# Attention and a feed-forward layer on one core: a planner in the kernel takes over the order of all engines

## The chip, the cores and the metric

The kernel runs on one core of one Trainium2 chip. Such a core has a matrix engine (TensorE, PE in the profile), three engines for everything else (VectorE is DVE, ScalarE is ACT, GpSimd is POOL), a queue engine (SyncE, SP) and 16 DMA engines that move data between HBM and the on-chip memories SBUF and PSUM. Each engine works through its own list of instructions in order and waits on semaphores for the others. The metric is the device time of one launch in microseconds (us), lower is better.

## The reference

Four sequences of 768 positions, eight heads of 64, go through masked attention; the result (3072 rows of 512) goes through a gated feed-forward layer. Heads 0, 2 and 6 see all earlier positions; the other five ("streaming" heads) see the first 4 positions and the last 64.

```python
scores = (q @ k.T) / 8                       # per batch and head, 768 x 768
mask   = causal                              if is_retrieval[head]     # [1,0,1,0,0,0,1,0]
         causal & (pos < 4 | rel < 64)       otherwise
a      = softmax(where(mask, scores, -1e9))
x      = (a @ v) as [3072, 512]
h      = x @ w_in                            # 512 -> 2048
out    = (h * sigmoid(beta * h)) @ w_out     # 2048 -> 512
```

All inputs and the output are f32 in HBM: q, k and v of 6.3 MB each, w_in and w_out of 4.2 MB each, the output of 6.3 MB.

## The kernel before

The work is cut in 8 chunks: a batch and half of its 768 positions, in the order (batch 0, first half), (1, first), (0, second), (1, second), and the same for batches 2 and 3. A chunk is counted from 0 here, so "chunk 1" is the second. Each chunk has four units, a pair of heads (p and p+4); unit u = 4 x chunk + p. Scores are computed in blocks of 128 keys by 128 queries, only where the mask lets anything through: 43 blocks in a chunk of a first half, 75 in one of a second half, 472 in all.

What happens to a chunk, with the lines of the profile:

- Loads. k, q and v of chunk 0, 1 and 2 come as f32 over SP's queue (`load_qk` L137, `load_v` L151). The weights come over POOL's queue, which casts f32 to bf16 on the way (L161 for w_in, L165 for w_out). From chunk 3 on, the rows of k and q come over POOL's queue too, cast on the way (`load_rows` L325, 60 loads); v stays on SP.
- Getting the head dimension onto partitions. Chunks 0 to 2: cast to bf16 (L293), transpose on PE (L367), copy out of PSUM (L368, L373). From chunk 3: a DMA transpose issued by SP (L336). `KT` holds the keys, `QTP`/`QTD` the queries. POOL makes a copy `KO` of the keys with the first 4 positions put in (L350, L351), and the same for the values, `VO` from `VX` (L312, L313). `VX` is the cast v (L299).
- Scores. Chunks 0 to 2 (`steps_QK`, L458) use a matmul over 128 rows with the other head's half of the queries zeroed; chunks 3 to 7 (`scores`, L926) use matmuls over 64 rows, the two heads side by side. Chunks 0 and 1 add the mask on PE (L463); later ones multiply it on DVE after the exponential (L431). The exponential is ACT's (L466, L930), into tiles `es`.
- Values. `steps_PV` (L489) multiplies `es` with `VX`/`VO`; DVE divides (L492, L494); the result `x` is transposed to `xT` on PE (L521, L523), or by a DMA from chunk 2 on (L505).
- Feed-forward. G1 (L554) is 16 tiles of 4 matmuls per chunk, each followed by a tanh on ACT (L557) and the gate on DVE (L560), which fills `gT`. G2 (L598, the last piece L581) is 12 parts of 4 matmuls per chunk; the result is scaled (L603, L605) and stored (L608).

The order is written out by hand: a list of calls for chunks 0 and 1, one loop for chunk 2 with a count of G1/G2 steps to put in, and from chunk 3 on a string per group of scores that says where G1 ("1"), G2 ("2") and PV ("p") steps stand. Loads have hand-set times. In the list for the start, chunk 1's k, q and v loads stand directly behind chunk 0's, ahead of the weights:

```python
    cast_dp(0)
    load_v(0, held=True)
    load_qk(1, 0)
...
    load_qk(1, 1, held=True)
...
    load_v(1, held=True)
...
    load_w_in(0)
```

`held=True` puts a small POOL memset into the tile ahead of the load, so that the load waits for it. PE starts with ten matmuls on zeros (`idle`, L188).

## Time and profile before

| what | value |
|---|---|
| median of 3 runs | 238.94 us (238.83 to 239.57) |
| span of the profiled execution, first to last instruction | 235.3 us |
| median less that span | 3.6 us |
| PE busy | 222.3 us (94% of the span) |
| ACT, DVE, POOL busy | 155.3, 144.7, 103.4 us |
| bytes read from HBM, written | 27.27 MB, 6.29 MB |
| granted TensorE clock | 1.00 throughout |

The page shows one execution, and of that the span; the page gives no total of its own for this execution, so the 3.6 us around the span is the distance to the median. Busy times of different engines lie beside each other. A busy PE counts a matmul from its start to its modelled end, so closely spaced matmuls overlap in it; what a matmul takes from the next one is read from the start of one to the start of the next.

### The profile page before, as it was taken

The page shows a single profiled execution, that of the slowest core. Times are in us where ns is not written, and L with a number is a line of the kernel's source. Part 1 is how long each engine was busy: PE and PEld are TensorE (multiplying, and loading weights), DVE is VectorE, ACT ScalarE, POOL GpSimd, SP SyncE. Part 2 cuts the span into 40 slices and gives each one's busy share as a digit, 9 for nine tenths or more (in the row PEclk, how much of TensorE's full clock was granted, in tenths as well). Part 3 has the DMA queues.
Part 4 walks back from the last instruction along what each step waited for, and adds up shares of the span by engine and source line. Part 5 has one row for each costly group of instructions (what it writes and reads, how often), then busy time and mean ns, then how long its engine had stood idle before and what let it go on. Part 6 is the DMA issues. An engine that isn't in the chain of part 4 may idle for free.

```text
span 235.3 us, 5334 instructions
## 1 busy us (share of the span) xinstructions
PE 222.3 (94%) x1960; PEld 131.8 (56%) x1960; DVE 144.7 (61%) x356; ACT 155.3 (66%) x303; POOL 103.4 (44%) x230
## 2 busy tenths in 40 slices
PE   7786899999999999999799999999989999999994
PEld 3675665555555566546454565455745556555553
DVE  6768679886758389637845592444881666338700
ACT  2796788847673998657674757584927797128621
POOL 6487850199469987059899319000560000000000
PEclk9999999999999999999999999999999999999999
DMA  6999999999999999989999963156511101211012
GB/s 196 261 276 194 177 167 231 224 212 212 201 133 132 129 139 156 148 146 150 219 192 142 212 149 81 46 92 165 123 33 61 49 0 45 81 45 49 0 45 89
DMA packets 96314, 31.78 MB, mean 135 GB/s; under 512 B 82704, under 2 KB 93344, under 8 KB 96288
## 3 DMA queue, kind: packets, MB, share of 16 engines
q0 software_dynamic: 35968, 8.13, 46.7%
q1 hardware_dynamic: 59456, 22.72, 45.0%
q10 hardware_dynamic: 864, 0.60, 0.8%
q8 instruction: 15, 0.25, 0.5%
q14 instruction: 11, 0.09, 0.1%
HBM read 27.27 MB, written 6.29 MB: 143 GB/s over the span
## 4 chain that ended last, share of the span: by engine, by line
PE 60%; DMA 14%; POOL 13%; DVE 4%; issue 3%; ACT 3%; SPq 2%; POOLq 0%; ACTq 0%
PE tp L598 25%; PE mm L554 21%; POOL s L325 7%; DMA vs<-in_v_dram 6%; DMA s<-in_q_dram 5%; PE po L489 4%; PE sp L926 3%; DMA xT<-x 2%; PE mm L188 2%; DVE gT L560 2%; POOL VX L299 2%; PE tp L581 1%; PE sp L458 1%; ACT es L930 1%; POOL KO L350 1%
## 5 line engine op out<-in xcount | busy, mean ns | idle before, releaser
L554 PE MATMUL mm<-xT,w_in_sb 128*128 128x384 bf16 x512 | 92.4, 326 | 1.5 <-DMA w_in_sb<-in_moe_w_in_dram 0.9
L598 PE MATMUL tp<-w_out_sb,gT 128*128 128x512 bf16 x368 | 89.6, 379 | 0.0
L557 ACT ACTIVATE th<-mm,beta_h 128x384 f32<-128x384 f32 x128 | 73.0, 597 | 24.0 <-PE mm L554 19.4
L560 DVE SCALAR_TENSOR_TENSOR gT<-th,mm 128x384 bf16<-128x384 f32 x128 | 67.7, 550 | 32.5 <-ACT th L557 28.1
L554 PEld LDWEIGHTS <-w_in_sb 128*128 128x128 bf16 x512 | 48.1, 97 | 33.9 <-issue 2.4
L598 PEld LDWEIGHTS <-gT 128*128 128x128 bf16 x368 | 33.8, 98 | 33.9 <-issue 0.8
L930 ACT ACTIVATE es<-sp 128x512 bf16<-128x512 f32 (+1 forms) x84 | 39.9, 597 | 4.1 <-PE sp L926 4.1
L605 ACT ACTIVATE osb<-tp 128x512 f32<-128x512 f32 x21 | 12.7, 604 | 35.4 <-PE tp L598 32.1
L299 POOL CAST VX<-vs 128x384 bf16<-128x384 f32 x22 | 11.4, 522 | 38.0 <-DMA vs<-in_v_dram 38.0
L489 PEld LDWEIGHTS <-es 128*128 128x128 bf16 x472 | 20.6, 97 | 10.8 <-issue 3.5
L466 ACT ACTIVATE es<-sp 128x512 bf16<-128x512 f32 (+1 forms) x44 | 22.7, 560 | 4.6 <-PE sp L458 3.6
L489 PE MATMUL po<-VX,es 128*128 128x65 bf16 x392 | 22.5, 193 | 1.0 <-POOL VX L299 0.9
L325 POOL DMA_DIRECT2D s<-in_q_dram x30 | 22.5, 773 | 0.9 <-issue 0.7
L431 DVE TENSOR_TENSOR es<-es,Mh 128x512 bf16<-128x512 bf16 (+3 forms) x58 | 19.9, 378 | 4.5 <-ACT es L930 3.8
L325 POOL DMA_DIRECT2D s<-in_k_dram x30 | 22.4, 775 | 0.5 <-issue 0.3
L494 DVE TENSOR_TENSOR x<-po,rec 128x384 bf16<-128x384 f32 x32 | 17.8, 557 | 1.1
L458 PE MATMUL sp<-QTP,KT 128*128 128x128 bf16 (+2 forms) x113 | 16.8, 230 | 1.7 <-ACT es L466 0.9
L350 POOL COPY KO<-KT 128x128 bf16<-128x128 bf16 (+1 forms) x24 | 10.2, 423 | 13.2 <-DVE KT L368 11.2
L431 DVE TENSOR_TENSOR es<-es,Mc 128x384 bf16<-128x384 bf16 (+2 forms) x21 | 7.2, 349 | 12.7 <-ACT es L930 12.0
L492 DVE RECIPROCAL rec<-po 128x6 f32<-128x6 f32 x32 | 6.1, 192 | 13.4 <-PE po L489 13.2
L458 PEld LDWEIGHTS <-KT 128*128 128x128 bf16 x113 | 10.4, 98 | 4.1 <-issue 1.2
L293 POOL CAST qkb<-s 128x384 bf16<-128x384 f32 x12 | 6.2, 532 | 13.4 <-DMA s<-in_q_dram 13.4
(73 smaller groups left out, 173.2 us busy)
## 6 DMA issues: line engine op xcount, KB each, us to landing
vs<-in_v_dram SPq DMA_DIRECT2D x24, 256.0 KB, 6.0
out_dram<-osb SPq DMA_DIRECT2D x23, 256.0 KB, 2.4
s<-in_k_dram SPq DMA_DIRECT2D x12, 192.0 KB, 4.8
w_in_sb<-in_moe_w_in_dram POOLq DMA_DIRECT2D x8, 256.0 KB, 7.6
w_out_sb<-in_moe_w_out_dram POOLq DMA_DIRECT2D x4, 512.0 KB, 10.9
s<-in_q_dram SPq DMA_DIRECT2D x10, 192.0 KB, 5.2
s<-in_k_dram POOLq DMA_DIRECT2D x30, 64.0 KB, 5.0
s<-in_q_dram POOLq DMA_DIRECT2D x30, 64.0 KB, 5.4
```

The costliest lines, as they stand in the source:

```text
L299: copy(out=VX[b % 2, p][:, h2 * HT:(h2 + 1) * HT, :, 0:D], in_=staged["v", c][:, :, p:H:NPAIR, :])
L325: nc.gpsimd.dma_start(out=ROWS[c % 2, name][:, t].rearrange("p (a w) -> p a w", a=NPAIR)[:, :, w:w + D], in_=src[b, hh * NPAIR:(hh + 1) * ...
L431: nc.vector.tensor_mul(e, e, m)
L458: nc.tensor.matmul(sp[:, (i - lo) * 128:(j - lo) * 128], lhs, s["QT"][hh][:, q0 * 128:(q0 + j - i) * 128], start=True, stop=not added)
L466: nc.scalar.activation(out=es[:, 0:w], in_=sp[:, 0:w], func=ACTF.Exp, scale=scale)
L489: nc.tensor.matmul(po[:, qi, hh, :], e, val, start=(j == 0), stop=(j == len(lst) - 1))
L494: nc.vector.tensor_mul(x, po[:, :, :, 0:D], rec.to_broadcast([128, HT, 2, D]))
L554: nc.tensor.matmul(hp[:, 0:HALF], w_in_sb[:, mo, fi * 128:(fi + 1) * 128], xT[c][:, mo, :], start=(mo == 0), stop=(mo == MO - 1))
L557: nc.scalar.activation(out=th, in_=hp[:, 0:HALF], func=ACTF.Tanh, scale=beta_h[:, fi:fi + 1])
L560: nc.vector.scalar_tensor_tensor(out=gTs[c][:, fi, :], in0=th, scalar=1.0, in1=hp[:, 0:HALF], op0=ALU.add, op1=ALU.mult)
L598: nc.tensor.matmul(op, gTs[c][:, fi, ns * 128:(ns + 1) * 128], w_out_sb[:, fi, :], start=(fi == 0), stop=(fi == FO - 1))
L930: nc.scalar.activation(out=es[:, 0:w], in_=sp[:, 0:w], func=ACTF.Exp, scale=scale)
```

## The change

The hand-written order is gone. All work is put into a list of tasks with an engine (or a choice of engines), a cost, what they depend on, a priority and the buffers they take; a `Planner` inside the kernel runs through them with its own clock while the program is built, gives each engine the first ready task in order of priority, and so writes a fixed list for every engine. The chip sees only the finished lists. The main parts:

- **Loads.** The order is a list, `ramp`: chunk 0, then all of w_in and a quarter of w_out, then chunk 1's k and q, a quarter of w_out, chunk 1's v, the rest of w_out, and then row after row of the later chunks. A tiny POOL copy (`hold`, L407) from a tile that landed into the destination of a later load makes that load wait. `kq` in the list is a unit's k and q.
- **Later rows as f32.** From chunk 2 on (`early` is 2), k and q come over SP's queue as f32 (L541), are cast by POOL or DVE (L251) and transposed by SP's DMA (L578). POOL's 60 casting loads (L325) are gone.
- **Scores over 64 rows everywhere** (L742), from chunk 0 on; the zeroed halves are gone. Masks of chunks 0 and 1 stay on PE (L731), now up to 384 columns in one matmul. Chunks 2 to 7 are cut in smaller groups.
- **Transposes.** PE transposes k, q only for chunks 0 and 1 (L512), and `x` only for those (L824); the rest goes by DMA (L832).
- **Buffers.** All 8 PSUM banks, 24 `es` tiles and 14 staging tiles of 128x512 f32 are handed out by the planner; v is cast in whole 128-row tiles by DVE or ACT, in chunks 0 and 1 also by POOL (L249, L251).
- **Attention ahead.** Groups of scores and PV have higher priority than G1 and G2; G2 is the filler. Both second-half chunks of batches 0 and 1 are through attention before chunk 2's G1 begins.

```diff
+CFG = {'fill': 10, 'g1_banks': (5, 4, 3, 2), 'long1': [0, 9, 18, 26, 34, 42], 'es': 24, 'early': 2, 'g1_limit': 1600, ...
+class Planner:
+    def pick(self, e):
+        kept = set()
+        lst = self.ready[e]
+        lst.sort(key=lambda t: t.prio if not callable(t.prio) else t.prio(self))
+        for t in lst:
+            if t.seen or t.ready > self.now:
+                continue
...
+            got = self.tokens(t, kept)
+            if got is not None:
+                return t, got
...
+    def hold(name, trigger, box, prio, make):
...
+            nc.gpsimd.tensor_copy(out=dst[0:n], in_=src[0:n])
+        return add("H" + name, "POOL", (124, 186), go, [trigger], prio=-500 + prio, take=box)
...
+        t = add(f"L{which}{u}", e_, 450 if e_ == "SP" else 400, go, [hd], prio=5 * u + (which == "q"),
+                take=box if hd is None else None, dma=(16, 40, *hw))
...
+    ramp = cfg.get("ramp", [("kq", 0), ("kq", 1), ("kq", 2), ("kq", 3), ("v", 0), ("in", 0), ("in", 1), ("in", 2), ("in", 3),
+                            ("out", 0), ("kq", 4), ("kq", 5), ("kq", 6), ("kq", 7), ("out", 1), ("v", 1), ("out", 2), ("out", 3)])
...
+    ramp = ramp + [x for c in range(EARLY, NCHUNK) for x in (("rows", c), ("v", c))]
...
-    def load_rows(c):
...
-            nc.gpsimd.dma_start(out=ROWS[c % 2, name][:, t].rearrange("p (a w) -> p a w", a=NPAIR)[:, :, w:w + D],
+                    eng[e].dma_start(out=s, in_=src[b, :, r:r + 128, :].rearrange("h p d -> p h d"))
...
+                def turn(e, which=which, t=t, box=box):
+                    j = h2 * HALF + t * 128
+                    out_ = KTB[b % 2][:, :, j:j + 128] if which == "k" else QTD[c % 2][:, :, t * 128:(t + 1) * 128]
+                    nc.sync.dma_start_transpose(out=out_, in_=box["w"].rearrange("p a c d -> p (a c d)"))
...
+            casts.append(add(f"Cv{c}{t}", cfg.get("v_cast", ("DVE", "ACT")) if c >= EARLY else cfg.get("v_cast0", ("DVE", "ACT", "POOL")), c_copy(512, False, True), go,
+                             [ld, t_ones[b % 2, h2]] + old, prio=u_prio(4 * c, -3), gives=[lambda ld=ld: ld.got]))
...
+        t = add(f"PV{u}", "PE", c_mm(65, nb), pv, ready_es[u] + vdeps, prio=prio, take=[(banks, 1, allowed, 1)],
...
+            t = add(f"G1.{c}.{fi}", "PE", c_mm(384, 4), mm, deps + w + old, prio=pr, take=[(banks, 1, cfg.get("g1_banks", (0, 1, 2, 3, 4, 5)), 1)])
...
-                    nc.tensor.matmul(sp[:, (i - lo) * 128:(j - lo) * 128], lhs, s["QT"][hh][:, q0 * 128:(q0 + j - i) * 128],
-                                     start=True, stop=not added)
+                nc.tensor.matmul(sp[:, a * 128:z * 128], lhs[half(h)], QTD[(u // NPAIR) % 2][half(h), units[u][2], q0 * 128:(q0 + z - a) * 128],
+                                 start=not st_, stop=True, skip_group_check=bool(st_))
```

Three places of the finished lists, on which the prediction rests.

POOL's list at the start. Before, POOL issues the first w_in load among the casts of chunk 1 (`qkb` is a cast k or q, `VO`, `VX` values of a batch, `s0` a staging tile); this is a stretch of before:

```order
L313 COPY VO00_154<-VX00_152 4x64
L161 DMA w_in_sb_78<-in_moe_w_in_dram 64x4x512 x2
L293 CAST qkb_400<-s0_200 128x384
L312 COPY VO01_157<-VX01_155 128x2x64
L313 COPY VO01_157<-VX01_155 4x2x64
```

After, w_in follows the last cast of chunk 0, and the one-column copies (L407) stand ahead of each load:

```order
L251 CAST qkb_255<-st_177 128x2x3x64
L407 CAST w_in_sb_69<-st_184 128x1 x2
L471 DMA w_in_sb_69<-in_moe_w_in_dram 64x4x512 x4
L609 COPY KO03_95<-KT0_87 128x128
L612 COPY KO03_95<-KT0_87 128x4
L407 CAST w_in_sb_69<-st_207 128x1
L471 DMA w_in_sb_69<-in_moe_w_in_dram 64x4x512 x2
```

w_in moved ahead of everything of chunk 1, and each of its loads now waits for an earlier landing.

PE's list where chunk 1's first values are used (`po` is PV's result, `VX10`/`VX1` the values of batch 1, `mm` G1, `sp` scores, `tp` here G2). Before, G1 of chunk 0 and scores of chunk 1 follow it:

```order
L489 LDWEIGHTS es_515
L489 MATMUL po_661<-VO10_164,es_515 128x65
L489 LDWEIGHTS es_515
L489 MATMUL po_661<-VX10_162,es_515 128x65
L554 LDWEIGHTS w_in_sb_78
L554 MATMUL mm_677<-xT_455,w_in_sb_78 128x384
```

After, all of chunk 0's G1 and all scores of chunk 1 stand ahead of it, and the first G2 stands behind this unit's twelve PV matmuls (these are the last scores, the first PV and, further on, the last PV and the first G2):

```order
L742 MATMUL sp_792<-QTD1_86,KT1_88 128x128
L742 LDWEIGHTS KT1_88
L742 MATMUL sp_794<-QTD1_86,KT1_88 128x128
L798 LDWEIGHTS es_758
L798 MATMUL po_809<-VX1_90,es_758 128x65
```

```order
L798 LDWEIGHTS es_749
L798 MATMUL po_809<-VX1_90,es_749 128x65
L798 LDWEIGHTS es_765
L798 MATMUL po_809<-VX1_90,es_765 128x65
L923 LDWEIGHTS gT_472
L923 MATMUL tp_825<-w_out_sb_70,gT_472 128x512
```

G1 and the scores moved ahead of the first use of chunk 1's v, and no G2 stands between its last score and that use.

DVE's list where the masks of chunk 2 start (`Mc`, `Mh1` are masks). Before, the casts of chunk 3's v stand after nearly all masks of chunk 2:

```order
L431 TENSOR_TENSOR es_1369<-es_1369,Mh1_146 128x512
L299 CAST VX10_162<-vs_833 128x6x64
L299 CAST VX11_165<-vs_833 128x6x64
L299 CAST VX12_168<-vs_833 128x6x64
L299 CAST VX13_169<-vs_833 128x6x64
L431 TENSOR_TENSOR es_1393<-es_1393,Mh1_146 128x512
```

After, the first of them (`st_1130` is chunk 3's v) stands ahead of the first mask:

```order
L942 TENSOR_SCALAR osb_1196<-tp_922 128x512
L251 CAST VX1_90<-st_1130 128x8x64
L771 TENSOR_TENSOR es_1245<-es_1245,Mc_80 128x384
L771 TENSOR_TENSOR es_1248<-es_1248,Mc_80 128x256
L251 CAST VX1_90<-st_1151 128x8x64
L771 TENSOR_TENSOR es_1282<-es_1282,Mc_80 128x128
```

The cast, and with it the wait for a load of chunk 3, moved ahead of the masks of chunk 2.

## The prediction

> **What bounds the kernel now.** I read the page's head and busy times, then the busy time by stretches, then the chain of waits for the pace of each kind of matmul, then the loads.

> ```profile
> span 235.3 us, 5334 instructions
> PE 222.3 (94%) x1960; PEld 131.8 (56%) x1960; DVE 144.7 (61%) x356; ACT 155.3 (66%) x303; POOL 103.4 (44%) x230
> ...
> 0.00:36.00 36.00, 30.03 (x359) 21.55 (x360) 25.83 (x75) 25.94 (x54) 23.60 (x78) 1.00 1.08 212
> 36.00:84.00 48.00, 47.14 (x398) 27.73 (x397) 35.01 (x80) 34.75 (x68) 31.70 (x55) 1.00 1.32 180
> 84.00:132.00 48.00, 46.33 (x428) 26.84 (x423) 30.77 (x79) 32.84 (x64) 34.60 (x66) 1.00 1.84 170
> 132.00:180.00 48.00, 46.86 (x402) 26.41 (x401) 27.29 (x67) 31.86 (x65) 13.49 (x32) 1.00 0.46 104
> 180.00:232.00 52.00, 51.89 (x387) 29.30 (x385) 25.48 (x55) 29.61 (x56) 0.00 (x0) 1.00 0.12 43
> ```

> In a row by stretches stand the stretch, its length, the busy time of PE, PE's weight loads, DVE, ACT and POOL, then clock, DMA share and GB/s. From 36 us on PE is idle for 3.8 us of 196; no other engine comes near. Before 36 us it is idle for 6.0, and what is busy there is thin: 359 instructions, many of them small. So the kernel is PE's work plus what the start loses. The start waits for data: the DMA share is over 1 there.

> The chain gives what one matmul takes from the next (its columns: start, length, what):

> ```profile
> 1.29 4.45 PE mm L188 x10
> 65.95 0.33 PE tp L367 x6
> 188.96 4.55 PE mm L554 x28
> 199.54 0.52 PE po L489 x17
> 221.65 6.91 PE tp L598 x32
> 228.55 3.51 PE tp L581 x32
> ```

> G1 162.5 ns (4.55/28), G2 216 ns and in its last half-width piece 110 ns, PV 30.6 ns, a transpose 55 ns. For scores over 64 rows the sum over all stretches serves, since two run side by side: these 254 matmuls hold 311 blocks, 11.86 us, so 38.1 ns a block, with the starts of the groups in it. Over 128 rows a block takes one 128-column matmul, 55 ns.

> ```profile
> sum 236.00, PE 11.86; mean PE 0.59
> ...
> 21.23 0.22 PE L458 MATMUL sp<-QTP,KT 128*128 128x128 bf16 x1
> 21.29 0.22 PE L463 MATMUL sp<-Ns,idb 128*128 128x128 bf16 x1
> 21.34 0.22 PE L458 MATMUL sp<-QTP,KT 128*128 128x128 bf16 x1
> ...
> 0.00:36.00 36.00, 7.62 (x42) 1.00 1.08 212
> ```

> The last row is G1 alone: 42 of 512 matmuls lie in the first 36 us. PE's list shows what else remains then: all of G2, 386 PV, 24 + 9 transposes, the 75 blocks of chunk 2 over 128 rows and all 311 over 64. By the paces above: 470 x 0.1625 = 76.4, 368 x 0.216 + 32 x 0.110 = 83.0, 386 x 0.0306 = 11.8, 33 x 0.055 = 1.8, 75 x 0.055 = 4.1 and 11.9, together 189.0 us. The last matmul ends at 228.55 + 3.51 = 232.06, so 196.06 us were spent on it: 7.1 us are stalls, spread out.

> **The change, part by part.** I set the end of PE's work after the change as the time of one event, plus the work behind it, plus stalls. The event is PE's first PV of chunk 1: it needs chunk 1's v, the last load that the start needs in full, and nothing can pass it in PE's list.

> *When chunk 1's v is there.* The rates of the loads are in four stretches of the start: k and q of chunk 0 at 3 to 7 us, v at 8 to 11, weights alone at 28 to 30 and, with the passage from w_in to w_out in it, at 28 to 35.

> ```profile
> 4.08 0.55 DVE L293 CAST qkb<-s 128x384 bf16<-128x384 f32 x1
> ...
> 3.00:7.00 4.00, 3.44 (x14) 1.61 (x13) 3.02 (x19) 0.93 (x4) 2.30 (x15) 1.00 1.09 338
> 8.00:11.00 3.00, 2.48 (x45) 2.31 (x43) 2.53 (x6) 2.52 (x6) 1.44 (x6) 1.00 1.32 220
> 28.00:35.00 7.00, 6.71 (x82) 4.78 (x83) 5.25 (x13) 6.06 (x13) 4.58 (x11) 1.00 1.13 171
> 28.00:30.00 2.00, 1.81 (x29) 1.54 (x30) 1.39 (x5) 1.79 (x5) 1.88 (x6) 1.00 1.20 193
> ...
> vs<-in_v_dram SPq DMA_DIRECT2D x24, 256.0 KB, 6.0
> w_in_sb<-in_moe_w_in_dram POOLq DMA_DIRECT2D x8, 256.0 KB, 7.6
> w_out_sb<-in_moe_w_out_dram POOLq DMA_DIRECT2D x4, 512.0 KB, 10.9
> s<-in_q_dram SPq DMA_DIRECT2D x10, 192.0 KB, 5.2
> xT<-x SPq DMA_TRANSPOSE x21, 4.1
> ...
> 100.56 3.89 SPq L336 DMA_TRANSPOSE KT<-s  x3
> ```

> The weights' sizes are those of the bf16 side (8 x 256 and 4 x 512 KB make 4.2 MB for 8.4 MB of f32), and so is their rate. The first k of chunk 0 is there at 4.08. Seven more loads of 192 KB at 338 GB/s take 4.1 us, v 0.79 MB at 220 takes 3.6: 11.8 us, as before the change. Then w_in and half of w_out, 3.15 MB: 16.3 us at 193, 18.4 at 171; I take the middle, 17.3, since passages from one queue to the other occur here too. Chunk 1's k and q 1.57 MB 4.7 us, its v 3.6. That is 37.4 us (36.4 to 38.5). The casts of v and POOL's copies for the first unit cost 0.5 + 0.24 + 0.3 + 0.23: PV of chunk 1 starts at 38.7. Overlap between the queues gains nothing here, the engines being full in each of these rows.

> PE has 64 G1 matmuls (10.4), 86 blocks (3.3), masks (68 blocks of columns, 3.7), 60 transposes (3.3), 43 PV (1.3) and the ten on zeros (4.45) to do until then: 26.5 us of 37.4. It waits some 11 us in the start, where the kernel before had no such wait but had less behind it.

> *The work behind that event.* G1 448 x 0.1625 = 72.8, G2 83.0 as before, PV 429 x 0.0306 = 13.1, 12 transposes 0.7, 386 blocks x 0.0381 = 14.7: 184.3 us. Relative to before, the 64-row scores of chunks 0 to 2 take away 161 x (55 - 38) ns = 2.7 us and 33 transposes 1.8 us. In their place SP issues nine more DMA transposes (six of chunk 2's k and q, three of x), 1.3 us each (3.89 for three), and 36 row loads instead of 8 unit loads and POOL's 60; 60 transposes then hold SP for 78 us of 230, which bounds nothing by itself.

> *Stalls.* 7.1 us before. In 84 to 132 stand 1.67 us of idle PE beside a POOL that is busy for 34.6 of 48 us; the chain goes through its casting loads there:

> ```profile
> L325 POOL DMA_DIRECT2D s<-in_q_dram x30 | 22.5, 773 | 0.9 <-issue 0.7
> L325 POOL DMA_DIRECT2D s<-in_k_dram x30 | 22.4, 775 | 0.5 <-issue 0.3
> L299 POOL CAST VX<-vs 128x384 bf16<-128x384 f32 x22 | 11.4, 522 | 38.0 <-DMA vs<-in_v_dram 38.0
> ```

> These 44.9 us go; 36 casts of 512 columns come, by the casts above (522 ns for 384) about 25 us shared with DVE. I let the 1.67 us go. New waits come with the order: DVE's and ACT's casts of chunk 2's v stand amid the gates and tanhs of chunk 1, those of chunk 3's v ahead of chunk 2's masks. Bounds: nothing, if the loads are early, and 6 us (the third rival). I take 1.0, near the low end, since G2 parts without these waits stand between. Stalls: 7.1 - 1.7 + 1.0 = 6.4.

> *Costed at nothing:* the masks of chunks 0 and 1 (same columns, fewer matmuls); `x` of the last unit by DMA, whose landing (4.1 us median before) is covered by the 52 G1 and G2 matmuls of older chunks (10.4 us) ahead of chunk 7's G1, and would cost its 4.1 without them. The last store is as before.

> *Sum.* 38.7 + 184.3 + 6.4 = 229.4 against 232.06: 2.7 us less. From the span of 235.3 that is 232.6, and with the 3.6 us around it (238.94, the median, less the span) 236.3 us. Its own range: 36.4 to 38.5 for v, 3 to 8 for the stalls, 233.0 to 238.0.

> **The rivals.**

> *The start and the order are better than I think.* Weights at 193 GB/s put PV at 37.7, and if a plan with one clock for all engines leaves 3 us of stalls, the end is 37.7 + 184.3 + 3.0 = 225.0, 7.1 less: 231.9 us. For it: no engine but PE is over 66% busy. Against: the stalls before are many and small, and the finished lists cannot give way to a late load.

> *The clock.* The first ten matmuls of 512 columns took 4.45 us, where 32 later ones took 6.91: ten would be 2.2. So a matmul after a pause at the start is at half pace, for 2.3 us in all. The longest wait of PE in the trace afterwards is 0.93 us, and no slow stretch follows it. After the change 11 us of waiting collect before 38.7, most in one piece; if the pace falls again, 2.3 us come on top: 238.6, no change. [...]

> ```profile
> 23.16 1.14 PE L554 MATMUL mm<-xT,w_in_sb 128*128 128x384 bf16 x6 [0.93 <-DMA w_in_sb<-in_moe_w_in_dram]
> ```

> *Slower: chunk 3's v is late.* Place: DVE's cast of it, ahead of chunk 2's masks; behind it wait the masks, behind these PE's PV of chunk 2. After v of chunk 1 (37.4) come the rest of w_out (1.05 MB, 5.8 us at 182), k and q of chunk 2 (1.57 MB at 220: 7.1), its v (3.6), six transposes (0.13 MB each at 220: 3.6), k and q of chunk 3 (7.1) and one v (1.2): 65.8. PE comes to PV of chunk 2 after 108 G1 and G2 matmuls (64 + 44, 19.9 us), 55 small ones (2.0), chunk 2's scores (2.9) and 36 G2 (7.8): 71.3. Ten masks (378 ns) and a cast lie between, about 4 us, so 1.5 us are to spare. The loads decide it when they take 30 us instead of 28.4. For it: with both kinds of load moving, 146 GB/s in 60 to 72.

> ```profile
> 60.00:72.00 12.00, 11.55 (x119) 7.39 (x118) 8.04 (x19) 8.07 (x17) 6.62 (x12) 1.00 1.41 146
> L431 DVE TENSOR_TENSOR es<-es,Mh 128x512 bf16<-128x512 bf16 (+3 forms) x58 | 19.9, 378 | 4.5 <-ACT es L930 3.8
> ```

> At a quarter more, 35.5 us, the masks are 5.6 us late, and the end is 241.9. Against it: that row is of POOL's small casting loads, which are gone.

> **How the numbers follow.** The forecast, 236.3, has 0.42; the better start, 231.9, 0.18; the clock, 238.6, 0.15; the late v, 241.9, 0.25. Within 0.3% of 238.94 (238.2 to 239.7, about what a measurement of this kernel can tell from no change) lies only the clock: faster 0.60, same 0.15, slower 0.25. The range reaches from 230.9, a microsecond under the better case, to 241.9, the late case; what is left out is the half of the late case that is later still and a few chances in a hundred below.

> **What would show it.** The first PV of chunk 1 (L798 on VX1) at 38.7, ended by a DMA or by POOL's copies behind it; PE's busy time in the first 36 us well below 30; G1 at 162.5 ns right after, or at 325 if the clock fell; scores (L742) at 38 ns a block; waits of DVE for a v load between 50 and 70 us; and PE idle for under 2 us from 90 us on. I am wrong if PV of chunk 1 comes before 36 or after 41, if the blocks of the small groups take over 45 ns (2.7 us more), or if PE waits in the late stretches, for which I have put in no new reason.

## The result: 268.53 us, and the profile after

The changed kernel takes 268.53 us (median of 4 runs, 266.29 to 272.62) against 238.88 for the kernel before, run beside it (238.51 to 239.57): 1.121 times as long, 95% interval 1.114 to 1.127. The forecast was 236.3. The profiled execution is the longest of the four, 272.62 us with a span of 270.9 and the lowest mean clock (0.937, the others 0.949 to 0.967), so the losses read from it below are some 4 us larger than those of the median.

The head of the page, and from its slices the clock that was granted to PE:

```profile
span 270.9 us, 5159 instructions
PE 233.2 (86%) x1873; PEld 129.5 (48%) x1895; DVE 136.1 (50%) x340; ACT 158.5 (58%) x317; POOL 71.7 (26%) x205
...
PEclk9999689599999597999999995999799999999999
```

Every other engine is busy for less or about the same as before, and PE for a smaller share. Two things are new: PE has holes, and the clock falls in six places. By stretches (PE, weight loads, DVE, ACT, POOL, then clock, DMA share, GB/s):

```profile
0.00:36.00 36.00, 27.93 (x214) 14.38 (x214) 17.63 (x53) 20.68 (x44) 19.62 (x70) 0.91 0.98 198
36.00:84.00 48.00, 42.23 (x328) 22.99 (x332) 22.29 (x48) 29.23 (x63) 19.95 (x50) 0.93 0.85 164
84.00:132.00 48.00, 40.05 (x384) 23.97 (x381) 27.16 (x72) 29.80 (x61) 13.35 (x36) 0.89 0.84 174
132.00:180.00 48.00, 39.82 (x305) 21.10 (x309) 25.84 (x68) 28.45 (x56) 16.93 (x44) 0.93 0.92 170
180.00:232.00 52.00, 48.08 (x468) 28.23 (x473) 34.03 (x85) 36.16 (x72) 1.86 (x6) 0.97 0.27 60
232.00:271.00 39.00, 35.13 (x193) 18.82 (x193) 9.16 (x17) 14.15 (x25) 0.00 (x0) 1.00 0.15 55
```

Before, PE was idle for 1 to 2 us in each middle stretch; now for 6 to 8. The last matmul ends at 267.2 instead of 232.06, 35.2 us later, and this divides as follows. PE's idle time up to its last matmul is 267.2 - 233.2 = 34.0 us, where it was 232.06 - 222.3 = 9.8: 24.2 us more. In half-microsecond stretches, 34.1 us after the start-up have a granted clock of 0.50; PE is busy for 28.0 us of them, which is 14.0 us of work at full clock, so 14.0 us are lost there, and none before. 24.2 + 14.0 is 38.2; the 3.0 us less are roughly the work that the change takes away.

What PE waited for, longest sums first (total, times, longest):

```profile
PE mm L856 <- DVE gT L864: 7.3, 5, 4.1
PE mm L856 <- DMA xT<-x: 5.5, 4, 2.6
PE po L798 <- POOL VX L251: 4.1, 1, 4.1
PE tp L512 <- POOL qkb L251: 3.6, 1, 3.6
PE sp L742 <- DMA QTD<-rb: 2.5, 1, 2.5
```

Behind the lower four stands a transfer, and behind the longest wait for a gate too. One place shows how a late load stops DVE, ACT and PE; the timeline at 158 to 169 us (start, length, engine, what, and in brackets the idle time before):

```profile
156.58 1.85 DVE L864 SCALAR_TENSOR_TENSOR gT<-th,mm 128x384 bf16<-128x384 f32 x3
163.02 0.43 DVE L251 CAST VX<-st 128x512 bf16<-128x512 f32 x1 [4.59 <-DMA st<-in_v_dram]
163.96 1.44 PE L856 MATMUL mm<-xT,w_in_sb 128*128 128x384 bf16 x4 [4.13 <-DVE gT L864]
164.00 1.05 ACT L861 ACTIVATE th<-mm,beta_h 128x384 f32<-128x384 f32 x2 [4.86 <-DVE gT L864]
...
157.86 1.69 SPq L945 DMA_DIRECT2D out_dram<-osb  x1
159.60 2.13 SPq L453 DMA_DIRECT2D st<-in_v_dram  x3
```

DVE's next instruction is the cast of a v tile. SP issues that load only at 159.60, behind a run of transposes and a store. The gates behind the cast had their tanh; G1 behind the gates had its inputs; all wait, and 4.1 us later PE goes on at half clock (0.50 from 163 to 169 us).

### The profile page after: what moved, and what is told of

Read it like the earlier page. It is cut to its first block, busy times and chain, and to the rows that moved or that the text cites. A ratio compares the mean times of both kernels' runs of the same rounds, so it can differ in the third digit from the quotient of the medians.

```text
span 270.9 us, 5159 instructions
## 1 busy us (share of the span) xinstructions
PE 233.2 (86%) x1873; PEld 129.5 (48%) x1895; DVE 136.1 (50%) x340; ACT 158.5 (58%) x317; POOL 71.7 (26%) x205
## 4 chain that ended last, share of the span: by engine, by line
PE 61%; DMA 20%; POOL 4%; DVE 4%; issue 3%; ACT 3%; SPq 3%; POOLq 0%; DVEq 0%; ACTq 0%
PE tp L923 25%; PE mm L856 24%; DMA st<-in_v_dram 10%; DMA xT<-x 5%; PE po L798 5%; PE sp L742 4%; PE mm L336 2%; DMA w_in_sb<-in_moe_w_in_dram 2%; DMA st<-in_q_dram 2%; ACT es L756 1%; DMA out_dram<-osb 1%; DVE gT L864 1%; SPq L453 1%; DVE x L812 1%; DMA QTD<-rb 1%
## 5 line engine op out<-in xcount | busy, mean ns | idle before, releaser
L923 PE MATMUL tp<-w_out_sb,gT 128*128 128x512 bf16 (+1 forms) x378 | 89.4, 379 | 4.3 <-ACT osb L940 2.5
L756 ACT ACTIVATE es<-sp 128x384 bf16<-128x384 f32 (+2 forms) x144 | 63.1, 532 | 9.1 <-PE sp L742 8.7
L923 PEld LDWEIGHTS <-gT 128*128 128x128 bf16 x400 | 38.1, 100 | 44.3 <-issue 8.1
L251 POOL CAST rb<-st 128x512 bf16<-128x512 f32 (+1 forms) x44 | 23.4, 545 | 45.9 <-DMA st<-in_k_dram 30.4
L940 ACT ACTIVATE osb<-tp 128x512 f32<-128x512 f32 (+2 forms) x19 | 10.8, 569 | 31.6 <-PE tp L923 24.0
L798 PE MATMUL po<-VX,es 128*128 128x65 bf16 x392 | 22.5, 206 | 4.9 <-POOL VX L251 4.1
L798 PEld LDWEIGHTS <-es 128*128 128x128 bf16 x472 | 20.7, 107 | 11.7 <-issue 7.5
L742 PE MATMUL sp<-QTD,KT 64*128 64x128 bf16 (+2 forms) x310 | 22.0, 241 | 4.2 <-DMA QTD<-rb 2.5
L771 DVE TENSOR_TENSOR es<-es,Mh 128x384 bf16<-128x384 bf16 (+3 forms) x60 | 20.3, 376 | 1.8 <-ACT es L756 1.3
L812 DVE TENSOR_TENSOR x<-po,rec 128x384 bf16<-128x384 f32 x32 | 17.6, 551 | 4.2 <-DMA xT<-x 3.7
L742 PEld LDWEIGHTS <-KT 64*128 64x128 bf16 x310 | 12.2, 96 | 14.3 <-issue 11.8
L942 DVE TENSOR_SCALAR osb<-tp 128x512 f32<-128x512 f32 (+1 forms) x7 | 4.4, 633 | 23.8 <-ACT osb L940 18.3
L640 POOL COPY VO<-VX 128x128 bf16<-128x128 bf16 (+3 forms) x24 | 8.9, 391 | 26.8 <-DVE VX L251 15.7
L251 DVE CAST VX<-st 128x512 bf16<-128x512 f32 x16 | 7.0, 447 | 14.9 <-DMA st<-in_v_dram 14.8
L798 PE MATMUL po<-VO,es 128*128 128x65 bf16 x80 | 10.7, 213 | 0.6 <-POOL VO L643 0.5
## 6 DMA issues: line engine op xcount, KB each, us to landing
st<-in_v_dram SPq DMA_DIRECT2D x24, 256.0 KB, 4.6
out_dram<-osb SPq DMA_DIRECT2D x23, 256.0 KB, 2.2
st<-in_k_dram SPq DMA_DIRECT2D x18, 256.0 KB, 5.0
st<-in_q_dram SPq DMA_DIRECT2D x18, 256.0 KB, 5.2
w_in_sb<-in_moe_w_in_dram POOLq DMA_DIRECT2D x8, 256.0 KB, 7.0
w_out_sb<-in_moe_w_out_dram POOLq DMA_DIRECT2D x4, 512.0 KB, 6.9
st<-in_k_dram SPq DMA_DIRECT2D x8, 192.0 KB, 3.8
st<-in_q_dram SPq DMA_DIRECT2D x7, 192.0 KB, 4.0
```

The lines of the kernel that those rows point to most:

```text
L251: eng[e].tensor_copy(out=out, in_=in_)
L742: nc.tensor.matmul(sp[:, a * 128:z * 128], lhs[half(h)], QTD[(u // NPAIR) % 2][half(h), units[u][2], q0 * 128:(q0 + z - a) * 128], start=n ...
L756: nc.scalar.activation(out=es[:, 0:w], in_=sps[n_][:, 0:w], func=ACTF.Exp, scale=scale)
L771: nc.vector.tensor_mul(x, x, m)
L798: nc.tensor.matmul(po[:, qi, hh, :], e_, val, start=(j == 0), stop=(j == len(lst) - 1))
L812: nc.vector.tensor_mul(x, box["po"][:, :, :, 0:D], box["rec"].to_broadcast([128, HT, 2, D]))
```

## The experiments

Four theories were weighed, and they changed as the runs came in. W: loading the weights ahead of chunk 1 costs the time, in the start. S: SP's queue is full, and what it issues is late (S2 is the same with the two kinds of its work told apart: row loads one behind the other, and transposes behind them). D: the DMA engines are full, or the landing of 256 KB rows is the limit. P, formed after the first four experiments: the lists were laid out for loads cheaper than the chip's, so that each list asks for data before it is there. C goes with all of them: a wait is followed by a stretch at half clock, as at the six falls above, of 3.4 or 6.8 us each.

For S, the issues of SP from 48 to 192 us, summed over the trace: 54 loads of 0.98 us, 54 transposes of 1.29 us, 13 stores of 0.70, 132 us of 144. A piece of SP's timeline:

```profile
120.95 4.87 SPq L541 DMA_DIRECT2D st<-in_q_dram  x3
125.92 3.08 SPq L453 DMA_DIRECT2D st<-in_v_dram  x3
129.10 4.11 SPq L578 DMA_TRANSPOSE KT<-rb  x3
133.31 3.84 SPq L578 DMA_TRANSPOSE QTD<-rb  x3
```

**The loads on POOL's queue.**

```diff
-'late_q': 'SP'
+'late_q': 'POOL'
```

> One setting of the changed kernel is altered: the f32 rows of k, q and the v tiles of chunks 2 to 7 are issued on POOL's queue instead of SP's; bytes, casts and transposes stay. Theory S (from 48 to 192 us the SP queue itself is full: its issues sum to about 132 of 144 us there, 54 loads for 54 us and 54 transposes for 68 us, and PE waits for what SP is late with): the loads' 54 us leave SP, the transposes alone fill under half of it, most of PE's 22 us of idle after 48 us and of the half-pace behind it go: 243 to 252 us. Theory D (the DMA engines or the landing times of 256 KB f32 rows are the limit, whichever queue issues them): 264 us or more, and PE's waits after 48 us stay. Both expect the first PV of chunk 1 where it was, near 44 to 48 us.

Measured: 276.04 us (268.69 to 279.89), no gain, since even the shortest run equals the changed kernel. The number lies in D's range, but what happened is in neither theory. SP was rid of the loads, but POOL now sent them out far ahead, chunk 3's among them, while SP's transposes of chunk 2 went out, and these landed late (the last column is from issue to landing; 48 to 84 us):

```profile
KT<-rb SPq DMA_TRANSPOSE x3, 17.6
QTD<-rb SPq DMA_TRANSPOSE x3, 10.7
```

In the changed kernel the medians are 2.6 and 2.4 us in that stretch. PE waited 18.5 us for `QTD` in two pieces. What is clear: freeing SP's issue time does not by itself bring data sooner. S in its plain form is out; D isn't shown by it, since the order of the transfers changed as well.

**x transposed on PE in all chunks.**

```diff
+'x_pe': tuple(range(8, 32))
```

> The changed kernel with x of all chunks transposed on PE instead of by DMA (24 DMA transposes less on SP, 72 PE transposes and 24 evictions more). Theory S: 24 x 1.24 = 30 us leave SP between 95 and 230 us, and xT no longer stands behind row loads; PE pays 72 x 0.055 = 4.0 us: 250 to 260 us. Theory D: the waits for v and k, q rows stay, only the 5.5 us of PE waiting for xT goes against 4 us of PE work: 264 to 269 us.

Measured: 264.05 us (262.61 to 264.62), 4.5 less than the changed kernel; it lies at D's edge, 264. SP's transposes between 48 and 192 us fell from 54 to 36 and all its issues there from 132 to 105 of 144 us, but PE's idle time in that stretch only from 21.5 to 20.0 us. So PE's waits stay when SP's queue is no longer full. It waited 5.6 us for gates, and for exponentials that stand ahead of what it needs on ACT 5.5 us in G1 and 4.4 in scores.

**The old order of the first loads.**

```diff
+'ramp': [chunk 0, kq 4 to 7, v 1, w_in 0 to 3, w_out 0 to 3]
```

> The changed kernel with the old order of the first loads: chunk 1's k, q and v directly behind chunk 0's, the weights after them. Theory W (the weights ahead of chunk 1 cost the time): v of chunk 1 lands near 24 instead of 47 us, both long waits of PE in the start go (3.6 and 4.1 us) with the half clock behind them (some 5 us): 254 to 259 us. Theory S: the rows of chunk 2 still start only behind the weights, near 47 us, and what PE gains ahead of them it waits for later: 263 to 269 us.

Measured: 265.65 us (264.64 to 266.64), 2.9 less, inside S's range and far from W's. The start did what W said:

```profile
23.23 0.52 PE L798 MATMUL po<-VX,es 128*128 128x65 bf16 x12 [0.36 <-ACT es L756]
```

PV of chunk 1 starts at 23.2 instead of 43.6 and doesn't wait for v. But of those 20 us 3 arrive at the end: PE waits for `QTD` (7.3 us), `xT` (5.7) and others later. The weights' place is not where the loss is, as long as the middle is as it is.

**PE kept at work in two waits.** 13 matmuls on zeros ahead of the first transposes and the first PV of chunk 1:

```diff
+    def warm_pe(bank, n):
+        for _ in range(n):
+            nc.tensor.matmul(bank, zeros[:, 0:128], zeros, start=True, stop=True)
...
+                if u == 4 and which == "k":
+                    warm_pe(tile_, 13)
...
+            if u == 6:
+                warm_pe(bank, 13)
```

> The changed kernel with 13 matmuls on zeros (13 x 0.216 = 2.8 us) put ahead of the first transposes of chunk 1 and ahead of the first PV of chunk 1, where PE waits 3.6 and 4.1 us for loads; they do no work of the computation. Theory C (after a wait of about 3 us the clock is halved for some 6.5 us more): the waits stay, but the granted clock is 1.00 from 26 to 53 us where it was 0.50 for 13 us, and PE is some 4 us further at 54 us. For the end theory S says that PE then only waits longer for SP's rows: 265 to 269 us; if the late stretches are bound by PE, 262 to 265 us. If C is wrong the clock falls all the same.

Measured: 267.54 us (265.92 to 268.69), 1.0 less, with overlapping ranges: at the end nothing that can be told from no change, as S said of the end. C holds: the clock in 0 to 36 and in 36 to 84 us is 1.00 where it was 0.91 and 0.93, and the first fall of the profiled execution comes at 97. What was won was lost again later: in three of the four runs the mean clock is 0.948 to 0.954, no higher than in the changed kernel.

So most of what PE gains, it waits for later; giving SP less to do or the start its data brings only 4.5 and 2.9 us. What these kernels share are the lists. The planner counts 450 ns of SP for a load that holds SP for 0.98 us on the mean in the trace (0.43 to 0.57 for four that stand alone, at 90.74, 111.76, 143.02 and 145.41). That led to theory P and to the next four.

**The planner's prices, and nothing else.**

```diff
-        x = add(f"Lv{c}{t}", qe, 450 if qe == "SP" else 760, go, [hd], ...
+        x = add(f"Lv{c}{t}", qe, 1150 if qe == "SP" else 760, go, [hd], ...
-                ld = add(f"L{which}{c}.{t}", qe, 760 if qe == "POOL" else 450, load, [hd], ...
+                ld = add(f"L{which}{c}.{t}", qe, 760 if qe == "POOL" else 1150, load, [hd], ...
-                tt = add(f"D{which}{c}.{t}", "SP", 1190, turn, ...
+                tt = add(f"D{which}{c}.{t}", "SP", 1270, turn, ...
-            T_X[u] = add(f"XD{u}", "SP", 1190, turn, ...
+            T_X[u] = add(f"XD{u}", "SP", 1270, turn, ...
```

> The changed kernel with other prices in its planner and nothing else: a row or v load from chunk 2 on occupies SP for 1150 ns instead of 450, a transpose for 1270 instead of 1190, as the trace shows them. The same instructions, in another order. Theory P: the lists of PE, ACT and DVE then put G1 and G2 where the rows are not there yet; of the 22 us of idle PE after 48 us two thirds go, and the clock falls fewer times: 247 to 256 us. Theory S2 in its strict form (SP is the bound whatever the order): 263 to 269 us, SP full until 190 us.

Measured: 254.65 us (252.59 to 256.14), 13.9 less, ratio to the kernel before 1.070 (1.064 to 1.077). P's range held; strict S's did not. (The first of these lines holds for every v load on SP, chunks 0 and 1 too.) The same stretch from 48 to 192 us, of the changed kernel and then of this one:

```profile
48.00:192.00 144.00, 122.52 (x1048) 69.03 (x1063) 77.54 (x199) 86.28 (x172) 49.09 (x129) 0.92 0.86 168
```

```profile
48.00:192.00 144.00, 132.98 (x1105) 73.28 (x1104) 87.50 (x211) 96.75 (x190) 43.09 (x109) 0.95 0.80 165
```

PE's idle time there is halved, 21.5 to 11.0 us (P had two thirds of it gone), at the same rate of the DMA engines, and the clock falls three times after the start-up instead of six. SP's issues of that stretch sum to 112 us instead of 132: the loads, no longer one directly behind the other, take 0.71 us each instead of 0.98 (0.53 to 0.60 from 125 to 143 us). And DVE waits for v less, first in the changed kernel, then here:

```profile
DVE VX L251 <- DMA st<-in_v_dram: 14.8, 6, 4.6
```

```profile
DVE VX L251 <- DMA st<-in_v_dram: 5.5, 2, 2.8
```

What the run doesn't part: a higher price puts PE's, ACT's and DVE's work elsewhere in their lists, and it also spaces the loads. And 1150 ns is about the pace of loads back to back (nine from 118.72 to 129.00 us in the changed kernel, 1.14 us each), above the 0.71 us that they take here on the mean, so the lists now have room to spare. No run tried a price in between, or the spacing alone.

**Casting loads again.** The k and q rows of chunks 2 to 7 by POOL's casting loads, straight into the tile that is transposed; POOL's and DVE's 36 casts go. There are 14 such tiles (`rb`) instead of 6.

```diff
+                        for cc in range(2):
+                            x = cc ^ pos(b, 0)
+                            nc.gpsimd.dma_start(out=o[:, cc], in_=src[b, x * NPAIR:(x + 1) * NPAIR, r:r + 128, :].rearrange("h p d -> p h d"))
+                    ld = add(f"L{which}{c}.{t}", "POOL", 1540, load, ...
+                             take=[(rb_p, 1, range(cfg["rb"]), 1)], dma=(64, 24, *sw))
```

> The part 'later rows as f32' undone alone: in the changed kernel the k and q rows of chunks 2 to 7 come over POOL's queue again, cast on the way (72 loads of 64 KB on the bf16 side); v and the transposes stay on SP. Theory S2 (SP's queue from 48 to 192 us is filled by two kinds of work one behind the other: row loads, which leave at the DMA engines' pace of 1.15 us each, and transposes at 1.25 us): 36 loads x 1.15 = 41 us leave that queue, and a transpose stands behind 18 v loads instead of 54 loads: 245 to 255 us. Theory P (the finished lists are laid out for loads that take 0.45 us of SP, the chip takes 1.1, and PE waits at one place after another, whatever brings the rows): casting loads are late as well, 260 us or more.

Measured: 253.09 us (250.68 to 256.22), 15.4 less; S2's range, and not P's 260 or more. But the casting loads stand in the planner at 1540 ns and with a slower flow of packets, so the lists were also laid out for later data, and the run with new prices gains 13.9 with the f32 rows kept. How much of the 15.4 is the casting load itself stays open; the f32 rows need not be given up.

**New prices with other parts undone.** Three kernels, each with the prices above: with the old order of the first loads; with that and x on PE; with chunk 2's k and q loaded by unit and transposed on PE (`'early': 3`).

> The changed kernel with SP's measured prices and the old order of the first loads, nothing else. With the old prices the old order of loads gave 2.9 us, since what the start gained was waited for later. If the lists now hold, the start's whole gain comes through: PE's 1.4 + 1.0 us of idle and the half clock behind them, and G1 and PV of chunk 1 earlier: 244 to 250 us against 254.65 with the new prices alone. If the middle bounds it all the same: 252 to 255 us.

> The new prices of SP, the old order of the first loads and x transposed on PE in all chunks, together, in the changed kernel. If the three causes (P, W and the 24 transposes of x on SP) add up: the x on PE alone gave 4.5 us, the old order of loads 2.9, P some 12: 246 to 252 us. If the loads' own time bounds the middle whatever the order: 258 us or more.

> The new prices of SP, and chunk 2's k and q loaded by unit (8 loads of 192 KB instead of 6 of 256 KB) and transposed on PE as before the change, in the changed kernel. SP loses 6 transposes and gets shorter loads there: about 10 us less SP work at the start of its full stretch. Theory S2: 5 to 10 us less than the run with the new prices alone. Theory P alone: within 3 us of that run.

Measured: 248.29 (247.01 to 250.67), 243.28 (241.42 to 244.41) and 244.30 us (242.85 to 251.92), the first inside P's range, the second 2.7 us below its own, the third 10.3 below the run with the prices alone, a little past S2's 5 to 10 and not with P alone. The old order of the first loads is worth 6.4 us now, 2.9 with the old prices; x on PE 5.0 on top. So with the new prices these parts bring more; that SP's work is the reason is not shown for chunk 2 by unit, where SP's issues over the whole run fall by 6 us (142 to 136) and PE gains 10.3. In the profiled execution of the second the clock never falls after the start:

```profile
PEclk9999999999999999999999999999999999999999
```

**All together, with the new and with the old prices.** New prices, old order of the first loads, chunk 2 by unit, x of chunk 3 on PE, row casts on POOL, v casts also there, `'fill': 6`, more slack for the loads, 16 staging tiles instead of 14 and a higher `'g1_limit'` (how much of ACT's work may stand ahead before G1 gives way); and the same settings with the planner's old prices.

> What the runs so far point to, in one kernel: the planner with the measured prices of SP's work, the old order of the first loads, chunk 2's k and q by unit and on PE (early 3), x on PE for chunk 3, the row casts of later chunks on POOL alone, those of v also on POOL, smaller stock of G2 in hand (fill 6). The new prices gave 13.9 us, chunk 2 on PE another 10.3 beside them; the old order of loads takes the 3 to 5 us of waits and half clock out of the start. Theory P: the lists now fit the loads, no wait of PE over 1 us and no fall of the clock after 10 us: 232 to 238 us. If the waits have only been moved, 241 us or more.

> The same kernel as the one before it in every setting, but with the planner's old prices (450 ns of SP for a row or v load, 1190 for a transpose): the same instructions, ordered by prices the chip doesn't keep. Theory P: 8 to 16 us above the other, PE idle and the clock falling again. If the gain of the other lies in its settings and not in the prices: within 3 us of it.

Measured: 241.15 us (12 runs, 238.28 to 242.46), ratio to the kernel before 1.008 (1.004 to 1.013), and 264.90 (6 runs, 264.26 to 267.36). Nothing but the prices lies between: 23.8 us, more than P's 8 to 16. That is the clearest result of the study. The stretch from 48 to 192 us, with the new and then with the old prices:

```profile
48.00:192.00 144.00, 139.91 (x1256) 78.28 (x1271) 90.67 (x217) 99.95 (x200) 56.09 (x134) 0.98 0.79 157
```

```profile
48.00:192.00 144.00, 123.20 (x1167) 69.53 (x1181) 87.90 (x212) 93.02 (x188) 56.18 (x133) 0.93 0.77 152
```

PE is idle for 4.1 us there against 20.8, and the DMA engines move about the same.

The first kernel lies 3 us above its range, at the case in which a wait has been moved, and its profile says which. The longest wait left, 4.0 us, begins at 42 us, for chunk 2's first k, which came in beside the last of w_out, with half clock behind it; another, of 2.2 us, stands at 95.

**That wait filled.** 14 matmuls on zeros ahead of chunk 2's first transposes, as above with `u == 8`.

> The kernel best_b with 14 matmuls on zeros (14 x 0.216 = 3.0 us; they do no work of the computation) ahead of chunk 2's first transposes, where PE waits 4.0 us for k at 42 us and runs at a granted clock of 0.50 from 47 to 51 us. Theory C with a price: the wait stays, the clock stays at 1.00, the 4 us at half pace become 2, and what is gained there stays, since PE waits only once more (2.2 us at 95): 1.5 to 2.5 us below best_b, 238.7 to 239.7 us. If the time at half pace is given back at the next wait: within 0.5 us of best_b.

Measured: 239.45 us (12 runs, 237.69 to 242.42), 1.7 less, inside C's 1.5 to 2.5. The ranges overlap almost wholly and the ratios to the kernel before, 1.004 to 1.013 and 0.998 to 1.006, in part, so the gain at the end fits C but is at the edge of what these runs can tell. The clock in the stretch itself is clear. The kernel without and then with the filling, each by a row of the timeline and one of the stretches:

```profile
46.42 0.34 PE L512 MATMUL tp<-idb,qkb 128*128 128x128 bf16 x3 [4.01 <-POOL qkb L251]
```

```profile
48.00:50.00 2.00, 2.00 (x10) 0.99 (x9) 0.56 (x1) 1.02 (x3) 1.08 (x3) 0.50 1.25 218
```

```profile
42.75 3.19 PE L336 MATMUL tp<-zeros 128*128 128x512 bf16 x13
46.36 0.34 PE L518 MATMUL tp<-idb,qkb 128*128 128x128 bf16 x3 [0.42 <-POOL qkb L251]
```

```profile
48.00:50.00 2.00, 2.00 (x19) 1.38 (x18) 1.70 (x4) 2.00 (x5) 1.27 (x4) 1.00 1.25 235
```

The transposes start at the same moment; in 48 to 50 us 19 matmuls start instead of 10.

**The remaining prices too.** Packets of the weights at 84 ns instead of 75, the landing of SP's loads at 2.2 us instead of 1.55, x on PE for chunks 2 and 4, `'fill': 4`. Other values moved with them: a unit's load from chunk 2 on at 600 ns instead of 450, `'g1_limit'` 900, 8 `rb` tiles, less slack for SP's loads.

> As best_b, with the prices of the weights' loads (84 ns a packet instead of 75) and the landing of SP's loads (2.2 us instead of 1.55 behind the issue) set by the trace of best_b too, smaller stock of G2 (fill 4), x on PE for chunks 2 and 4 instead of 3. Theory P: the 4.0 us wait at 42 us, for k rows that landed behind the weights, and the half clock behind it go, so that what is left differs little from the forecast for best_b: 234 to 239 us. If the wait is moved and not filled: 240 to 243 us.

Measured: 238.09 us (12 runs, 236.03 to 239.34), ratio to the kernel before 0.9997 (0.996 to 1.003): the same. PE's longest waits, beside those of the changed kernel above:

```profile
PE po L798 <- DVE x L812: 2.3, 1, 2.3
PE mm L336 <- DVE zeros L330: 1.3, 1, 1.3
PE sp L742 <- DMA QTD<-rb: 1.1, 2, 0.9
```

The planner's order, with the first loads and chunk 2's k and q as before the change, is then as good as the one by hand. Which of the values moved here did it stays open. No version that beats both was found.

## Why the prediction was wrong, step by step

**The event, 38.7 us.** v of chunk 1 landed at 38.9, 40.9 and 47.4 us, not at 37.4. The chain of waits shows the last tile, and the timeline what stood beside it:

```profile
37.70 9.67 DMA st<-in_v_dram
47.42 0.62 POOL VX L251
```

```profile
35.62 2.61 SPq L453 DMA_DIRECT2D st<-in_v_dram  x3
37.12 1.49 POOL L480 DMA_DIRECT2D w_out_sb<-in_moe_w_out_dram  x2
48.08 0.38 PE L798 MATMUL po<-VX,es 128*128 128x65 bf16 x4 [4.06 <-POOL VX L251]
```

I put the second half of w_out behind v because the list names it there. The last two pieces go out on POOL's queue at 37.12 and 37.86, on both sides of the third v tile at 37.70, and all shared the DMA engines until 47 (share 1.03 and 180 GB/s from 37 to 47 us). The rest is the hand-over: k and q of chunk 1 were complete at 33.3, the first v load left SP at 35.62, after 5.2 us of SP waiting for POOL's one-column copies, which stood behind casts. My sum had no time for a hand-over. The first PV matmul started at 43.6 and the wait inside its unit ended at 48.1; both are past the 41 that I had named as the point where I am wrong. At 43.6 nothing waited for v: PE came straight from scores, late by its 3.6 us wait for k at 30 us and the half clock from 29.1 to 35.9. Only the third tile, at 48.1, is a wait for v.

**The work behind it, 184.3 us.** Right within 2.3 us. PE is busy for 197.7 us behind the event, 22.3 of them at half clock, which makes 186.6 at full clock. In the last kernel above, where the clock stays at 1.00, 386 blocks of scores from 32 us on take 15.81 us, 41.0 ns each against 38.1 put in (1.1 us more). In the changed kernel G1 takes 82.08 us behind the event instead of 72.8; most of that is the clock's.

**The stalls, 6.4 us. This is the term that failed.** From 43.6 to 267.3 us PE is idle for 223.7 - 197.7 = 26.0 us:

```profile
43.60:267.30 223.70, 197.71 (x1581) 110.91 (x1599) 113.09 (x276) 129.93 (x254) 49.67 (x129) 0.94 0.62 126
```

I had 229.4 for the last matmul, this execution has 267.3. Of the 37.9 us between them 4.9 lie in the event, 19.6 in the stalls, 11.1 in the clock behind the event and 2.3 in the work.

Three steps of mine lie in the stalls. "60 transposes then hold SP for 78 us of 230, which bounds nothing by itself": they came as forecast, 1.29 us each, but I counted them alone. With 54 loads and 13 stores in the same queue SP is at 132 of 144 us, and a v load stands behind them, as at 159.6 above. (The run with x on PE showed that this sum alone is not the bound.) "I take 1.0, near the low end" for casts of v amid the gates: DVE waited 14.8 us for v in six places, PE 7.3 us for gates. The place was right, the size was not. For the landing of x by DMA I priced only the last unit, "covered by the 52 G1 and G2 matmuls of older chunks". There it was covered; but PE waited 5.5 us for `xT` in four places, at G1 of chunks 2, 4 and 5, for which my sum had no term. I had seen that finished lists cannot give way to a late load, and used it only against the better rival. What stands in the place of this step is the planner's price: with SP's loads at the price of loads back to back, and nothing else but the small correction for the transposes, the kernel takes 13.9 us less, and 23.8 less in the other settings. Alone that is 13.9 of the 29.7 us between the two kernels; the rest went only with parts of the change undone beside it, above all the order of the first loads and chunk 2's k and q. The lists were written by a clock that takes 450 ns for a load; that number stood in the code, and in the trace of the kernel before SP's 17 loads from 48 to 192 us take 0.78 us each; I did not compare the two.

**The clock.** The rival was right in kind and too small: six falls and 14.0 us instead of one and 2.3. I had tied it to the one pause in the start. No trace ahead of the result showed a fall after a wait, and for the first ten matmuls (4.45 us) the granted clock reads 1.00 in the kernel before; at the six falls it reads 0.50. In the forecast itself the clock stood at nothing. Each stretch of half pace is paid on top of a wait that was already paid.

**The late v of chunk 3, 241.9.** The place was right: chunk 3's v landed from 78.8 us on instead of 65.8, DVE waited 4.4 us with chunk 2's masks behind it, and PE then 1.1 us for ACT, which had waited for the same v. The same happened with v of chunks 4, 5 and 6, ahead of gates, up to 163 us; a range of 230.9 to 241.9 had it as a single event.

**Chances.** "Slower" had 0.25, and each of the cases was one delay at a time. That they have one cause in large part, a plan whose loads are too cheap, and so come together, was missing. (The prediction's "own range" is also a little narrow: its bounds, 36.4 to 38.5 and 3 to 8, added end to end give 231.9 to 239.0, not 233.0 to 238.0. That changes nothing here.)

## What to carry to other kernels

When a planner or a table fixes the order of in-order engines, compare its price of every kind of transfer with the issue time and the landing time in a trace before anything else: here 0.45 us in the plan against 0.98 in the trace for one kind of load (and a small correction for the transposes) was worth 13.9 us with the other settings unchanged and 23.8 us in later settings; the best single part of the change that was undone gave 15.4. Count a queue by everything that it issues, stores and loads and transposes together, and by their spacing: the row and v loads of these lists held it for 0.98 us each on the mean where many went out back to back, and for 0.71 with the new prices, where they were spread out. And price a wait of PE with the half clock behind it (14.0 us in the changed kernel).

## What the runs showed of the hardware

In 0.2 us stretches of the changed kernel (PE's busy time, clock, DMA share, GB/s) a fall of the clock, its end, and the next ones:

```profile
29.00:29.20 0.20, 0.00 (x0) 0.71 1.35 319
35.80:36.00 0.20, 0.20 (x4) 0.72 0.56 87
46.00:46.20 0.20, 0.00 (x0) 0.88 1.24 241
52.80:53.00 0.20, 0.20 (x2) 0.55 1.09 206
87.00:87.20 0.20, 0.00 (x0) 0.78 0.31 57
93.80:94.00 0.20, 0.20 (x1) 0.65 1.27 278
```

A DMA transpose of 128x512 bf16 (131 KB) holds SP for 1.24 us (`KT`) and 1.21 us (`QTD`) in the changed kernel, medians of 18 each from 48 to 192 us; the 1.29 above is the mean with the 18 smaller ones of `x`. From 103.5 to 107 us SP issues them one behind the other and nothing else, and the DMA engines move 98 GB/s on the mean with a share of 0.51. In 40 slices of that stretch they are busy (in tenths) and move:

```profile
DMA  9998410000016999998310000016999998310000
GB/s 208 222 208 196 77 9 0 0 0 0 0 20 126 222 211 217 211 219 193 71 10 0 0 0 0 0 20 126 219 196 243 199 219 193 74 9 0 0 0 0
```

The full slices have 193 to 243 GB/s, and the engines are busy for about half of the time from one issue to the next. In the run with the loads on POOL's queue, 14 of which went out from 48 to 84 us, the transposes that SP issued in that stretch took 10.7 and 17.6 us to land (medians of three each) instead of 2.4 and 2.6; PE's 18.5 us of waiting for `QTD` in that run stand behind them.
